# Three constant tiles fetched by another queue, and a new order of all operations, in a windowed attention with a mixture-of-experts attention behind it

## The chip, the cores and the metric

The kernel runs on one core of a Trainium2 chip. The core has TensorE (PE: matmuls; PEld: loading of the stationary operand, which runs beside the matmuls), VectorE (DVE), ScalarE (ACT), GpSimd (POOL) and SyncE (SP), which here only issues transfers. The metric is device time of one execution in microseconds (us), the median of several runs.

## The reference

Two layers over 8 batches, 576 positions and 512 features. The first is attention with 8 heads of 64, a window of 128 positions back and a bias that falls with distance; its output is the input `x` of the second, in which 4 experts each project to 64, do causal attention over all 576 positions, project back to 512, and are summed by the weights of a gate that keeps the best two.

```python
scores = scale * np.matmul(q, k.transpose(0, 1, 3, 2))
mask = (rel >= 0) & (rel < window)                      # window = 128
scores = np.where(mask, scores + bias[None], -1000000000.0)
attn = softmax(scores); x = np.matmul(attn, v)          # then [B, S, 512]

logits = x @ w_gate; topk = best 2 of 4; w = softmax(logits[topk])
for e in range(4):
    q = x @ wq[e]; k = x @ wk[e]; v = x @ wv[e]
    a = softmax(np.where(causal, -1000000000.0, scale * (q @ k.transpose(0, 2, 1))))
    out += w_e * (a @ v @ wo[e])                        # only where e is in topk
```

## The kernel before, in words

The heads go in pairs; pair g belongs to batch g // 4. For each pair the kernel forms blocks of 128 queries against 256 keys: scores on TensorE (tiles `s`, for the first batch `sA`, `sB` and `sC`), mask on VectorE (`COPY_PREDICATED` from `mkt`), bias and row minimum on VectorE (`CUSTOM_DVE_ANT_0` from `tbt`), exponential on ScalarE (`ACTIVATE pA<-pA,nmA`), sums and reciprocals on VectorE (`r`), scaling by the reciprocal on ScalarE or GpSimd (`pA<-pA,r`), transposition on TensorE with the identity `idt` as an operand (`tA`, `tB`, `tC`, `t`), splitting of the transposed block by the mask `tmt` on VectorE together with a plain copy on ScalarE or VectorE (both into `paA`, `pa`), and the product with the values `vt` (`xA`, `xB`, `xt`). The result is kept as a rounded part and a remainder (`xh`). The second layer multiplies these with rounded weights `WH` and their remainders `WL` (`qk`, `v`), forms causal scores (`ms`, `msl`), transposes their exponentials with `idt` (`mt`), and so on to the output.

The four pairs of the first batch are a special case, so that work starts before whole rows have arrived. Their rows come in two halves. `fetch(g, m, 0)` (L313) fetches the first halves of queries and keys of m pairs from g on, one transfer of 128 KB for each of the two heads of a pair, into the tiles named `e`; in a listing these are `e<-in_hd 64x2x256`. One of them, of pair 0, is issued by ScalarE, the others by SyncE. `fetch(g, 2, 1)` and `fetch_tl` (L342) fetch the second halves and the tails of the queries of two pairs: `e<-in_hd 128x2x128`, `e<-in_hd 64x2x256`, `e<-in_rd 128x2x320`, `e<-in_hd 64x2x256`. `fetch_v` (L346) fetches values, `wload` (L991) a chunk of weights of 386 KB (`wst`), and for c = 4 the output weights `wo` of 512 KB and the causal bias `mtt` of 200 KB.

`half_units(0)` (L1206) emits the work on first halves: scores `sA`, probabilities `pA`, transposes `tA`, products `xA`. `half_units(1)` emits that on second halves: the tail scores `sC`, whose operands come from the transfer `e<-in_rd 128x2x320`, the scores `sB`, and what follows. `wprep` rounds weights beside it, and the first projections `qk` come right behind.

None of these calls issues anything. They record operations in a list (`_Rec`); an operation with two possible engines is recorded by `any()` with both. `plan()` (L158) then decodes a string of numbers, `ORDER`, each of which names an operation and which of its two engines takes it, and L1276 issues them in that order. So every operation has line 1276 in the profile, and the order within each engine is that of the string. A negative number stands for a fill: a matmul of a zero tile `QZm` into a scratch tile (`warm`), whose result nobody reads. The string before has 6482 entries, 13 of them fills.

Transfers that SyncE and ScalarE issue use eight semaphores in rotation, in the order of the string: before a transfer can be issued, the one eight places ahead of it must have landed. `tbt` is the bias tile, fetched by ScalarE at the start; `mkt[:, :P]` is computed from it by VectorE, `mkt[:, P:]` is fetched and used for the tail scores `sC` alone.

Of the kernel before, what the change touches and what calls it, by code (L numbers as in the profile page):

```python
# [21 lines left out]
E = 4  # L22
# [21 lines left out]
    "M{knlU;enW`?ZG?lAn6Gq9@&24)v~;9?K{UR@E+cn5@0hfIkteCV<kS27h@8)K-HlyQ3O>Gw;7Q*Bb8cDoYLaKlARd-1pPV8`&D80YI-a81*`>"
    "S|0`I3!aLF^LbWN>ipdF>av(oL>9q&+)z`O6iKN|&?vpWnMpWXUG}#fOepP&qb*xFEZhp1>pj-H?zeiB6Wt2&@qr32JkwQ}pCHNen7;ERaJ=x0"
    "Ei3P1FF>9rB~_(LQ-MONw)Y2MY{HQ<HUYVAw9&MT`39MJehJnkkpk~3fKr3*>h#rBN2ePJbEPl+FgK|*#hOr7YV(N8v<gFxBin9tW@>MEq|Pi%"
    "^L^p^;5aPW6sS{lV??PL9WwNEskM(k8R&<U#__)HzHUd3ZXdvC=$y(eeD7CpeP7aOAI$3qmb$ykp|b(?3|{ML?J(@8Dch#P^8@nUiLw2=zX{_i"
    "ID@D(FgDR22&d@pc&)o{J9*{t2Ub!<w|=bY{`a<AD;|&qb;hptgiuhM*yuF;;75rsK9}1#r_;NWEi>+g&8{36O3EvkV74^Mg;{gDVj(P39+!xV"
    "M~&Hmy+eD(QI)vRTII>j%6ibtmnV(t>P4f5nyr8TqLpbnKG2RsLGj?QBv)gp+gVTj!V^>B+!1qnrn6V$FYb1Vr^Y0U<D1221;s-xZF}9CbyaW2"
    "Z8x_^7He9f4M~1+Pf2+~-axc6(NL$;&s&S8nnR3aeg<H=Bo&TMg%kcx*$VUrRwlGCG@u#m2rf)(rG37!A>|X_t2p(ISd&vsTkGbkie%l?*81N+"  # L50
    ")dt}y<@&Cy5V^WW!7FX-PlaYpCB`dQYw8-6FALzLs#gobRcQb5FCg7yEh;T4wPk(sZ7^8U_M6Xw+Aq=RYkQNA8&&&t(T$3#GpMNg+kXp(@4kYN"
    "Kb%rNQ=L^(US87Iea7e~c}3+(k)h)=S)*~P2v(L3=K7jTG_yar(WpyJ-!EuRovKfk2y6WkAsp*5adgV8lBP_(T)aB1Q)!o{!k$+?nw%mUFLPN2"
    "oRDJ=PqlXe$n`lVOKYHus1q}9zGX%|?t+ofMtX3+<jIFr=IJ@u8-4A&*Y@{XG#(Hp<`*hYcVWID6}&#Mm9Gt^tVTD6MnN1@ZnY-C?>-fDWxJA+"
    "FMSH?o1mywmM6dY;l`GdawsWUs;D|RUfvl?kuaXLP)*V<IChHC%PL`gt8CiX+MkjC$d$Ibqdt$n0okyzB`u>lbG5lZ(VbNj$pv?R@KDn3*kZKK"
    "uvH_)LG|c#X!P1XOvB(X49F0X5<ri_1}rE;<)GHI>vq+r-7}L7{+7n6^}cTTlrU&)Fz&CI_Wc2!=yb*5S)jfytrfP(x?5cBuFMt)jt9qw6nXIc"
    "tIs{Q^!(pM60a|>3(BlZg|;l1EFNY=-F<dTMq_B?u);sK1A9|fuFr?&iKD;1WVfWs(ZV-(K62Z}NP_;PZ9P?|Qs-<$l^L3xez!>uZs@dnj1~~K"
    "fq!_g)SD=swDudTI{aDIe8u>sI~HoJfBsbY(M=B;6HR3vw+XfwPZAVaeBQ==$VjtB#4==4`K2$9udKCx=Zh)rGie!vjmD2YJAT%Yp!)e$XIkR)"
    "T&Xj6uFX+BXJ|Km?xlia{g)n!&b4-Aq)E1P1-|vx8F?WJ=l-@r-MGx}fJ~ljth&^?Rr9?+hGZx*$yL95-^xI5rg1lavTR~W&S;{hE$AJPBp6@%"
    "(ZMm8tVzjkZ^hFet<2T5qFB4pnJ{<574WW1&2|=VOI=0?C^dt_>Ma-=omKA4uWzMq4%iQ@J16R6{hVzi*_+!n=JW1shET*C%bZ<EMg|l53TFBW"
    "_BY+Vlf@--&^Pqo_mmt4ecsSmej#WFa{^XV3$rwzDRE?Mo^C|*dwBr)X01-2l>E@6@W=Z*vi0(PlgrTn*$8``J^g`P_k5tde;Vf8N=<*^iU#tn"  # L60
    "7%wLDK9Va7mxgPl*6u!|)@FBr^K<XZ(j{HFTAT@4Da#oRV?zN;r1`n8@43JCgAR+w)mUFRvb>`zV?<>WIo&xw{+SKz?ZYS-D%(+#eDS5U3`e7s"
    "_rlfT?4d424q8HEi&&QDfxICR9Kr#wP}iwJU`|b$?Ma=UtMA#>h7HP`q6Vm{y|z44Q&I0x-1zRjLzD!Ql83y$VebM=8V+H4uB7~j|5^$i_y2f#"
    "wd}5csgZUhj5D6@KFdyj@wNS4b7_6q;ctFl)@S2k<Qo)WTayNQI?c860+5<hj^Gqd98R?BgJX$!WerY_!=T#*HOfAB+-x;KkeP|1d~>=qzr-}p"
    "EVZ^YR{rYrDW#@~H~9g2a=h*G?GyFG>*IrwT<w8=X<itquGgwli;Gf@d%TN|+GexXZhh{KCO16$4Hzn{o@@7d_<tL%i44QZf4ptSHj)Fjt>OY3"
    "^bfT(j`lfr2ZyhPhesHR<MAiqy|>-=z0lqo=IYRtA;*v<b!ZNvk@hS{o-om!i<StG(I|C6o7~&h*lS&CZc96D9W;CA);F@R`SLW`Hb_H4LEQn~"
    ";XG}<HLF^0Jpg0FEIjgcIC<{Q>ACGpV|v#BOt+YqcVuhbBUMs+nSDO8q4PN;t!}f~Av<fa7p^~kXX<*+KfO5k&kt{E)xWH}ld<msG*^@#RE{+S"
    "$Ndc{sp0fdfSSI|88h<v=YJUXc_Fu|q<rs*&%s*KQcWbO%-k!v_R_Nf$@VVTvV>bawf1c4O6?CHxOv7N>RdA%kL-fM*lAW5YLqo*Fxg$%ND$2)"
    ";w<3@scU~VJS9w=Uz(m1%RnrXTh~xL+fH;WdDL@@<}}TwC_$>&+>xh*r@~E*wR?w?Galtk{om<^$&9<MSZcFAANh@Or!}+ZENWkxAK!50y3;aH"
    "^mWWNm3A6uqAEtDtSS7&rxr!6A9@}bn3>GEXY|WR=yWF|lJ@BV(s!lBkbUs`o8+njU8M&}0PjGrQ<OP1*`;=O?i<#a<fP;zt;Ux8t6u}4ZMJtI"
    "o&^pq_Jd=8p{um$`NwAc&df1r@A$|ECEyT+w^p<jBcA%lA5;XwSKld0hV3K?f}-e`U$vi2jo6{QB=B!v+RGY7;5j<YPH%y;QI}Ma-+v1BPPZ`8"  # L70
    "+Vsd{v+7+WA%FhTaxV<b>w7xO%rM^l*ds_LB}q0<^RvV<e*-dDZlzRNIppg9=6!AJ?yH|RDEx{U80ekV21Y_f6T`Xt-L|bgS6^?o3mDO~a|Lo7"
    "V$aFZF-lob?~@D;7yROB^kjW&Jp{oNeI69%gEn>a#F>-=V>VubOCA{<K7(-5mP8tcTmKY>2?+0+uD>jq40TlrgXr7Da&GIy2rNxQ$D$}Nd43+I"
    "R@)WQx-MyGe7mo^%?*G1v>m$L`H;E?;$&5F5p|1l>R;|39~{o}^amWu@`7T>t*dUcm6tTtPx4OeHkhmpPuVT}cSk)vJJF5*c=TFr(ZR7?1>2|g"
    "fHKEmbU07uuI<ZJ?YG~IRq_b0qdC`&vaA@g7E2DtHwP*j4ysyZV@j7Pw`<YWINQ7?pE<HERKxz+oJl;qrXCp3Ohfr*sN`qQns0xmuRT4{WZ6tM"
    "1x$srW}6$y$HX;brZdy$*tzsUOJ(HoUpO~=A~uoARyugO>&B9DEfP9?=?X2FRul%I;&4ne^0TKh%u$(g$1j8OtDjja%Wi{+RWbYYp8;0eE6YoQ"
    "n$0bxM!sQ|8<DV;M~^d8g<5&f`#%;aE`W#MpFTE`WA7b+ingup1+=FwPt$CA?M}g2ZKkE=#h+k7vAin&<#mRP)x25zMl>zsuq7zTYfef&s@gm3"
    "Pd@ThR82>B#&$QNM+oPQo@lx~CpnlZ=|Nhk9|lmE911D6VC3)LIdYDUA%B}{Bl(l3I^S7n1pe){)85$ykgFCWWtBJIvK{)1VBBont~VROaFjb|"
    "3@e&z@<Q1I*(s;$){I>F?3(LHyjD4L&3$09)G4y<Szv0TUM?RTlFoF9{f*izlqhVuz7t+`EwW~&GeLqqwYLJ#zc6$6m9N|j8})(yTHPS?LI3|v"
    "U-;T}{=lRvFu8;Hm6DpGL)h;<MHSFUZFP0>PzSV|B7kxw5?!12%-ymE$m_AJL6lcmhXmB-4u~_$_k+3abWP7se*u#-&26xLfYLe0)#m&KxK>*Q"
    "-~9H<T7U9Jb#1h1zx0kr{k!gU->flj+n#pAeb6ZCcE0ohm@dsfK4_|U_lKlTm2#n^T&j5f)(!CPwj7-{r%Y5-`6W(NouCQxJnExURR%a@N^o79"  # L80
    "P-_i^Gb174gU>8RwpFJ`d7k5ge95)b$&eZLLZXWNYa!9>-o$Kv`$R9m(@%kVE$s_W==4JaZGp5lUst!j3Z#l)X%kA7mb8d;Pvoer&a%DZv${Q%"
    "xa(Tt7C@^#r~i0#TIS$&ruc*7qeIp+p2>Q`J3SiDvT5Lf52ztj)~463`5U4ellT6i?Hy0%R>~&_(vtT~8za5h>E<QBNgQrj@D8i?h0|8BWPsBK"
    "!Yq4z$GF)6US7s>GE_C^FnzkoYAZA86g$Bet*DX=l`f?r6ck2!D~<Y-zLv;YWV*q=e8$u1yZdarLeHwyI_y6A$z^M*I9+8bO==x4DE$6^d3}td"
    "1TDOywX$Sp*0E-mYnNAHS=r|^B!X1)=Wjcen#G;tjRej9%YVXX-pOno-3}?FFy;=-Ht3rJ;i=6)Ye!Yof#zw>->o)gZSTJNxWYA%aNMI?TUiq="
    "mmGK3{qnU&xZxZ1D4WV#Iy<1I&O3bdJ=3T2(2z9}NX$gJX6<BRF+Hr<jvPi&E9v-+?^N7!Ge|N9wpB}j6!gm4vJYw3*|4gAZ+4<=eB5L2e(2H0"
    "joikKXlhN4B3EJEMBv?+?QGa;Ks2gv`pi93K~+z4n>b?n@=f~*l1wMeuaBxD_gx(xJluoJ-+`0C0Km7N<BmVnf~y|L->B6;@soqBX{104mlq?m"
    "J-tj5BoD4K47k%4W|QuH2|n}0E+POg6=lNc28LR9;JIfOt6c{5m7jyTBlC_Aj-ogPM-$`0o$A`{o*aBiFu!CAo}#?u$Vr&hAc_pwHk*bWcGNx7"
    ">3#SWK;mla=om7Yxh8n(X%rb2BlBu^m%+F#SzBIx_8HOgYScK4AU3+y3cB&2q5m}3t&_a}l2t6bwl6N~+9+#0mMXlyvex_mwW_nnU#3&Qo_2&M"
    "I^2_d<U`#py+QY8f~0K$)*pDK5+?J}>bH|eha#OlDelgisVYa3J0zT5%5`5u+3O5j<m^xq6)~AERQHbu_tTBnVAr7uPY6dQI(s@x%H^X8K2SDv"
    "{_~^NX(0xdBg-d|lhpE(g}!cgLE`CASGA{aR^P1=t__V2jg}-TKKX7?7bE=vSAY9~zxD@4P+hB9KieB`7dM$~y5Zmb;baO>?n9{#l7sjBpsb~H"  # L90
    "N{aL=D3hZn2D!5($U6zGx0S(3(n@hY9PXv2xIjGb@+O3|Q&L5y#hlsKon^}u?tbJE<Ci|%EL7Dtof&U^u-dnB@8+YULkUxv9SM?o<*B;vl~;>V"
    "MVD?UPnC}HIzv12OD1c7z+&$d7BjWC-}(5H{(-)f^1RwpuQBWNGY=wA!>upNl$vZ<EJn&==etjT{}1Wr^e_BkH*BArf#%)n+RaK?WqPm<w3~Xb"
    "v$F>@=(%07wr5+dDX(0duC!aU2Rbv{_-7fYL6Z<nU#c8}z0{cj_~fTMo!Q1c&zWl!qMc2$`K6<DV|dX6izn(rlXU|5!jW?vw#?NxA+(6Ckwr^r"
# [1270 lines left out]
```

## Time and profile before

| | |
|---|---|
| median of 3 runs | 545.17 us (545.03 to 545.23) |
| the profiled execution | 545.23 us |
| its span in the profile | 543.5 us, so 1.73 us lie around it |
| granted TensorE clock, mean over the span | 1.00 of full speed |
| busy: TensorE, VectorE, ScalarE, GpSimd | 532.0, 451.4, 424.7, 348.8 us |
| DMA moved | 72.99 MB, mean 134 GB/s |

The times of single instructions, waits and transfers are those of the profiled execution. "Busy" counts an engine as busy while an instruction runs on it; matmuls overlap each other, so the durations of successive rows can overlap too.

### The profile page before, as it was taken

How to read it: one execution, taken by the hardware profiler on the slowest of the kernel's cores; microseconds unless marked ns; L12 is line 12 of the kernel's file. 1: busy time of each engine (PE TensorE's matmuls, PEld its weight loads, DVE VectorE, ACT ScalarE, POOL GpSimd, SP SyncE). 2: the span in 40 equal slices, each digit the busy share in tenths (PEclk: the TensorE clock that was granted, in tenths of full speed). 3: DMA queues.
4: the chain of work that ended last, by engine and by line, in shares of the span. 5: the costliest groups of instructions: out<-in, count | busy, mean ns of one | idle time of the engine just before them, and what ended most of it. 6: DMA issues, size and time to landing. Idle time of an engine off the chain costs nothing.

```text
span 543.5 us, 13708 instructions
## 1 busy us (share of the span) xinstructions
PE 532.0 (98%) x4353; PEld 453.9 (84%) x4353; DVE 451.4 (83%) x1945; ACT 424.7 (78%) x1477; POOL 348.8 (64%) x591
## 2 busy tenths in 40 slices
...
GB/s 201 252 189 109 155 74 145 132 163 160 200 128 98 175 143 239 157 59 199 141 123 201 119 202 149 148 107 175 162 156 169 81 161 24 76 21 2 19 60 98
DMA packets 30376, 72.99 MB, mean 134 GB/s; under 512 B 3168, under 2 KB 11360, under 8 KB 30304
## 3 DMA queue, kind: packets, MB, share of 16 engines
...
q10 hardware_dynamic: 880, 0.59, 0.4%
q14 instruction: 37, 0.30, 0.2%
HBM read 62.67 MB, written 9.44 MB: 133 GB/s over the span
## 4 chain that ended last, share of the span: by engine, by line
PE 92%; DVE 3%; DMA 3%; issue 1%; SPq 0%; ACTq 0%; ACT 0%; DVEq 0%
PE qk L1276 19%; PE s L1276 11%; PE v L1276 10%; PE o L1276 9%; PE x L1276 8%; PE ms L1276 7%; PE mt L1276 7%; PE ma L1276 7%; PE t L1276 5%; PE msl L1276 2%; PE mal L1276 2%; PE xt L1276 1%; DMA e<-in_rd 1%; PE mtl L1276 1%; DVE pa L1276 1%; DMA tbt<-in_tb 1%
## 5 line engine op out<-in xcount | busy, mean ns | idle before, releaser
L1276 POOL TENSOR_TENSOR h<-r,h 64x512 fp32r<-64x512 f32 x96 | 122.9, 1282 | 16.7 <-DMA r<-in_rd 9.9
L1276 PE MATMUL qk<-xh,WH 128*128 128x288 f32 (+2 forms) x512 | 123.0, 312 | 0.4 <-DVE ot L1276 0.3
L1276 ACT ACTIVATE p<-p,nm 128x128 f32<-128x128 f32 x252 | 99.3, 396 | 14.4 <-DVE nm L1276 12.8
L1276 PEld LDWEIGHTS qk<-xh,WH 128*128 128x128 f32 x512 | 85.0, 189 | 5.2 <-issue 1.6
L1276 POOL TENSOR_SCALAR mp<-mp,mr,w 128x512 f32<-128x512 f32 (+3 forms) x128 | 76.1, 604 | 16.9 <-DVE mr L1276 9.8
L1276 ACT ACTIVATE mp<-mp,mnm 128x256 f32<-128x256 f32 (+3 forms) x128 | 71.1, 557 | 13.5 <-DVE mnm L1276 12.9
L1276 PE MATMUL qk<-xh,WL 128*128 128x288 f32 (+2 forms) x256 | 76.8, 307 | 0.0
L1276 PE MATMUL s<-h 128*128 128x256 f32 x336 | 72.8, 299 | 0.0
L1276 POOL TENSOR_SCALAR p<-p,r 128x128 f32<-128x128 f32 x131 | 47.4, 368 | 36.6 <-DVE r L1276 13.2
L1276 PE MATMUL ms<-KHm,QSm 128*128 128x256 f32 (+2 forms) x224 | 69.0, 359 | 0.1
L1276 DVE TENSOR_TENSOR pa<-t,tmt 128x512 f32<-128x512 f32 (+2 forms) x84 | 64.3, 773 | 5.6 <-PE t L1276 3.7
L1276 PE MATMUL v<-WH,xh 128*128 128x260 f32 x288 | 65.2, 294 | 0.0
L1276 ACT COPY mpt<-mt 128x384 f32<-128x384 f32 (+1 forms) x84 | 44.1, 534 | 26.6 <-PE mt L1276 25.1
L1276 PE MATMUL mt<-idt,mp 128*128 128x128 f32 x320 | 60.9, 273 | 0.0
L1276 DVE CUSTOM_DVE_ANT_0 mp<-ms,mtt 128x256 f32<-128x256 f32 (+2 forms) x96 | 52.4, 552 | 8.1 <-PE ms L1276 7.5
L1276 PEld LDWEIGHTS s<-h 128*128 128x128 f32 x336 | 53.3, 189 | 3.7 <-PE ma L1276 0.4
L1276 DVE CUSTOM_DVE_ANT_0 p<-s,tbt 128x128 f32<-128x128 f32 x204 | 53.2, 284 | 1.9 <-issue 0.2
L1276 PE MATMUL x<-pa,vt 128*64 128x256 f32 x448 | 51.6, 359 | 0.1
L1276 DVE COPY_PREDICATED s<-mkt,s 128x256 f32<-128x256 int32 (+2 forms) x140 | 45.0, 330 | 6.3 <-PE s L1276 4.4
L1276 PE MATMUL t<-idt,p 128*128 128x128 f32 x252 | 49.7, 273 | 0.1
L1276 PEld LDWEIGHTS v<-WH,xh 128*128 128x128 f32 x288 | 48.2, 189 | 1.9 <-issue 1.3
L1276 ACT ACTIVATE p<-p,r 128x128 f32<-128x128 f32 x121 | 45.4, 396 | 5.0 <-DVE r L1276 3.7
...
## 6 DMA issues: line engine op xcount, KB each, us to landing
...
tl<-in_hd SPq DMA_DIRECT2D x24, 64.0 KB, 3.4
...
```

The costliest lines, as they stand in the source:

```text
L1276: getattr(getattr(tc.nc, e), m)(*a, **k)
```

## The change

The three fetches of constants leave ScalarE's queue. `idt` (64 KB) is issued by SyncE between the fetch of pair 0 and those of pair 1 in the code, `tmt` (64 KB) behind the first halves of pairs 2 and 3, and `mkt[:, P:]` (32 KB) behind the last weight chunk. And the string `ORDER` is another one, for the whole program: 6477 entries, 8 of them fills, and with the same operations otherwise (6469 distinct ones in both). Some operations are on their other engine: three plain copies into `paA` in the first batch's first halves go to VectorE, and roundings of the weights `WH` to ScalarE in their place.

```diff
 ORDER = (
-    "c-pmjeOzl-m3GcKD<8LTO>Ck`P1>ZAX{bblB^_uJC#gvVZ_<J#l_<Fb78G7V!G@N!V1q&nQ>b7;!9s-!N=BH0npm(w!2yMzprFKp1_gx*dg%)m"
...
+    "c-pmje^_g0m2URlD?iRjG^wOFjG$1HHnC8XmQ0C;Hfh5&oRT(aVGIfiHYil6P@zrQ#DWC{1q(K@(1HgXXoH0gSTY3#4N4T0D2z}+;T9ZF7{P+V"
...
     zero()
     fetch(0, 1, 0)
     nc.scalar.dma_start(tbt[:, 3], tb[:, 3])
-    nc.scalar.dma_start(idt, ident)
-    nc.scalar.dma_start(tmt, tm)
-    nc.scalar.dma_start(mkt[:, P:], mk[:, P:])
     nc.vector.tensor_scalar(mkt[:, :P], tbt[:, 3, 0, :], -1.0e6, None, op0=ALU.is_lt)
...
     warm()
+    nc.sync.dma_start(idt, ident)
     fetch(1, 1, 0)
     fetch_v(0, 0)
     fetch(2, 2, 0)
+    nc.sync.dma_start(tmt, tm)
     fetch_v(1, 0)
     fetch_v(2, 0)
     wload(0)
     fetch_v(3, 0)
     for c in range(1, 4):
         wload(c)
+    nc.sync.dma_start(mkt[:, P:], mk[:, P:])
     aseq, marks = attn_units()
```

SyncE's queue at the start of the program, before. `e_107` holds the rows of pairs 0 and 1, `e_111` those of pairs 2 and 3; `vt_110`, `vt_112`, `vt_113` and `vt_115` are the values of pairs 0 to 3.

```order
L1276 DMA e_107<-in_hd 64x2x256 x3
L1276 DMA vt_110<-in_vd 128x256
L1276 DMA e_111<-in_hd 64x2x256 x4
L1276 DMA vt_112<-in_vd 128x256
L1276 DMA vt_113<-in_vd 128x256
L1276 DMA wst_114<-in_wall 128x772
L1276 DMA vt_115<-in_vd 128x256
L1276 DMA wst_116<-in_wall 128x772
L1276 DMA wst_117<-in_wall 128x772
L1276 DMA wst_118<-in_wall 128x772
L1276 DMA e_107<-in_hd 128x2x128
L1276 DMA e_107<-in_hd 64x2x256
```

The same place of SyncE's queue after, as far as the third of the moved transfers.

```order
L1276 DMA e_107<-in_hd 64x2x256 x2
L1276 DMA vt_110<-in_vd 128x256
L1276 DMA e_111<-in_hd 64x2x256 x4
L1276 DMA tmt<-in_tm 128x256
L1276 DMA vt_112<-in_vd 128x256
L1276 DMA vt_113<-in_vd 128x256
L1276 DMA wst_114<-in_wall 128x772
L1276 DMA vt_115<-in_vd 128x256
L1276 DMA wst_116<-in_wall 128x772
L1276 DMA wst_117<-in_wall 128x772
L1276 DMA wst_118<-in_wall 128x772
L1276 DMA mkt<-in_mk 128x64
```

Ahead of these rows stand one `e_107<-in_hd 64x2x256` and `idt`, and behind them the second halves `e_107<-in_hd 128x2x128` and so on as before. So SyncE issues three more transfers ahead of the first transfer of a second half. Further on, the transfers of the tail of a later pair (`tl`, 64 KB) and of `mtt` (200 KB) now stand ahead of most of the second halves of pairs 2 and 3, and `wo` (512 KB) ahead of the last values; before, they came behind these.

TensorE from the last block of the first half of pair 2 to the first projections, before. `tA_147` are the transposes of pair 3, `xA_145` the product of pair 2, `sC_163` and `sC_157` the tail scores of pairs 1 and 0, `sB` the second-half scores of pair 0.

```order
L1276 MATMUL sC_163<-e_107 128x192
L1276 MATMUL warm_109<-QZm 128x256
L1276 MATMUL sC_157<-e_107 128x192
L1276 MATMUL sB_0_155<-e_107 128x256
L1276 MATMUL sB_1_156<-e_107 128x256
L1276 MATMUL sB_0_155<-e_107 128x256
L1276 MATMUL sB_1_156<-e_107 128x256
L1276 MATMUL xA_145<-paA,vt_113 64x256 x2
L1276 MATMUL xA_145<-paA,vt_113 64x128 x2
L1276 MATMUL tA_147<-idt,pA_133 128x128 x4
L1276 MATMUL qk_0_0_165<-xh_131,WH 128x256 x2
```

The same place on TensorE after.

```order
L1276 MATMUL tA_147<-idt,pA_133 128x128 x4
L1276 MATMUL warm_109<-QZm 128x256 x3
L1276 MATMUL sC_163<-e_107 128x192
L1276 MATMUL warm_109<-QZm 128x256
L1276 MATMUL sC_157<-e_107 128x192
L1276 MATMUL sB_0_155<-e_107 128x256
L1276 MATMUL sB_1_156<-e_107 128x256
L1276 MATMUL sB_0_155<-e_107 128x256
L1276 MATMUL sB_1_156<-e_107 128x256
L1276 MATMUL xA_145<-paA,vt_113 64x256 x2
L1276 MATMUL xA_145<-paA,vt_113 64x128 x2
```

The four transposes `tA_147` moved from behind the scores `sB` to a place ahead of the tail scores `sC`, with three fills between; the first projections `qk` now follow the product `xA_145` directly. On VectorE the reciprocal for pair 3, by which `pA_133` is scaled ahead of these transposes, stood behind a rounding (`WH`) and a remainder (`WL`) of weights, and now follows directly on the sum that it is taken of.

## Rows read from the trace of the kernel before

**Rows 1.** The first part of the profile's page (busy time of each engine, its share of the span, number of instructions) and the shares by engine of the chain of work that ended last.

```profile
PE 532.0 (98%) x4353; PEld 453.9 (84%) x4353; DVE 451.4 (83%) x1945; ACT 424.7 (78%) x1477; POOL 348.8 (64%) x591
...
PE 92%; DVE 3%; DMA 3%; issue 1%; SPq 0%; ACTq 0%; ACT 0%; DVEq 0%
```

**Rows 2.** Busy time of each engine by stretch of the span (start and end of the stretch in us: its length, then for each engine its busy time and, in brackets, how many instructions; then the granted TensorE clock, the busy share of the 16 DMA engines and the GB/s that they moved).

```profile
10.00:15.00 5.00, 4.51 (x22) 3.26 (x20) 3.96 (x24) 3.94 (x18) 2.09 (x6) 1.00 0.93 305
15.00:20.00 5.00, 3.78 (x30) 2.74 (x31) 3.20 (x15) 4.13 (x19) 3.52 (x8) 1.00 1.11 283
20.00:25.00 5.00, 5.00 (x41) 3.57 (x40) 4.21 (x21) 3.74 (x16) 3.17 (x6) 1.00 1.04 263
...
60.00:80.00 20.00, 19.86 (x163) 16.46 (x164) 18.52 (x83) 15.71 (x63) 16.65 (x30) 1.00 0.25 76
80.00:100.00 20.00, 19.65 (x143) 15.46 (x145) 18.34 (x81) 17.68 (x65) 15.66 (x28) 1.00 0.60 197
100.00:200.00 100.00, 99.92 (x848) 87.59 (x844) 86.04 (x383) 82.86 (x285) 73.72 (x119) 1.00 0.44 145
200.00:300.00 100.00, 99.71 (x819) 85.49 (x816) 87.90 (x371) 84.91 (x293) 70.76 (x110) 1.00 0.49 155
```

**Rows 3.** Waits of TensorE over the whole span (engine, tile and line that waited, what it waited for: us in total, times, longest).

```profile
PE sA L1276 <- DMA e<-in_hd: 4.2, 1, 4.2
PE sA L1276 <- PE sA L1276: 0.8, 1, 0.8
PE sC L1276 <- DMA e<-in_rd: 0.7, 1, 0.7
```

**Rows 4.** Timeline of SyncE's queue from 0 to 25 us: start us, duration us of the row's issues together, the transfer, how many issues.

```profile
0.74 2.09 SPq L1276 DMA_DIRECT2D e<-in_hd  x3
...
3.50 3.94 SPq L1276 DMA_DIRECT2D e<-in_hd  x4
7.48 1.07 SPq L1276 DMA_DIRECT2D vt<-in_vd  x2
8.59 0.43 SPq L1276 DMA_DIRECT2D wst<-in_wall  x1
...
9.59 1.33 SPq L1276 DMA_DIRECT2D wst<-in_wall  x3
10.96 1.34 SPq L1276 DMA_DIRECT2D e<-in_hd  x2
12.35 0.59 SPq L1276 DMA_DIRECT2D e<-in_rd  x1
```

**Rows 5.** Waits of SyncE's queue from 0 to 25 us, columns as in rows 3.

```profile
SPq L1276 <- DMA tbt<-in_tb: 1.4, 1, 1.4
```

**Rows 6.** Timeline of ScalarE and its queue from 0 to 25 us: start us, duration us, instruction, count, and in brackets the idle time before it and what ended that.

```profile
6.20 0.34 ACTq L1276 DMA_DIRECT2D tmt<-in_tm  x1
6.58 0.44 ACTq L1276 DMA_DIRECT2D idt<-in_ident  x1
8.06 0.40 ACT L1276 ACTIVATE pA<-pA,nmA 128x128 f32<-128x128 f32 x1 [1.45 <-DVE nmA L1276]
...
12.99 0.33 ACTq L1276 DMA_DIRECT2D mkt<-in_mk  x1
13.87 0.37 ACT L1276 COPY paA<-tA 128x256 f32<-128x256 f32 x1 [0.70 <-PE tA L1276]
...
20.05 0.99 ACT L1276 ACTIVATE pA<-pA,r 128x128 f32<-128x128 f32 x3 [0.51 <-DVE r L1276]
```

**Rows 7.** Timeline of TensorE's matmuls from 0 to 25 us, columns as in rows 6.

```profile
15.85 1.09 PE L1276 MATMUL warm<-QZm 128*128 128x256 f32 x7
...
19.82 0.56 PE L1276 MATMUL sC<-e 128*128 128x192 f32 x2 [0.69 <-DMA e<-in_rd]
...
20.76 1.13 PE L1276 MATMUL sB<-e 64*128 64x256 f32 x8
...
22.62 0.66 PE L1276 MATMUL tA<-idt,pA 128*128 128x128 f32 x4
23.04 0.48 PE L1276 MATMUL qk<-xh,WH 128*128 128x256 f32 x2
```

**Rows 8.** Timeline of TensorE's weight loads from 0 to 25 us, columns as in rows 6.

```profile
5.94 0.50 PEld L1276 LDWEIGHTS sA<-e 64*128 64x128 f32 x2 [0.81 <-DMA e<-in_hd]
6.63 1.40 PEld L1276 LDWEIGHTS sA<-e 64*128 64x128 f32 x8 [0.20 <-DMA e<-in_hd]
```

**Rows 9.** Timeline of VectorE from 0 to 25 us, columns as in rows 6.

```profile
10.79 0.16 DVE L1276 TENSOR_REDUCE r<-sm 128x4 f32<-128x8 f32 x1 [0.91 <-ACT pA L1276]
...
18.79 0.16 DVE L1276 TENSOR_REDUCE r<-sm 128x4 f32<-128x8 f32 x1 [1.08 <-ACT pA L1276]
...
20.78 0.35 DVE L1276 COPY_PREDICATED sC<-mkt,sC 128x64 f32<-128x64 int32 x2
```

**Rows 10.** From the view of the tile wst (the weight chunks), 0 to 40 us: the time from issue to landing of its four fetches.

```profile
DMA to landing us min/median/max: 4.4/5.1/6.4
```

**Rows 11.** From the view of all DMA issues: destination and source, queue, number of issues, KB each, median us from issue to landing.

```profile
tl<-in_hd SPq DMA_DIRECT2D x24, 64.0 KB, 3.4
...
mtt<-in_mt SPq DMA_DIRECT2D x1, 200.0 KB, 3.1
```

More of the change, by code (lines that the diff above doesn't have):

```diff
@@ L44 @@
[L44 to L93, printed above, removed]
@@ new lines @@
+    "2nx#mzHjdU=ZyDx=KgW>gd}J0Z+}15df&C)wT=!z1>}|L66sT2DWz!!O<ihwZ>mev6-srP8L3+3s#Oh1tFtrqd!^OlLy5ao3%S}Mv3V^RpS|WT"
+    "?ow}fAOCQDeA~(Gj}+Ib;Qf4kLQz@o6Zg5=!CUK)R=&)8I?p3@`JQ+r|J@Illte5+(Dmm_(vMTW@ca{RHye*X@N>)YeeY!WVE(kYzSVd6wqJfA"
+    "#XA7-&8J`H@m@*EzU}@QXY*0Zqkk*Z>Sqh}9i^WyzQbLbs&EG;RSnH80dMWMzjx|shCh5-_rM#uSxHt~b<T}nXx*0F#INhrg?sB{ZJkDQQ)~Kf"
+    "o{5%K0<5~03?8fbOE1KgYxmyqdW$aAH{bfu2lLcL&=Sb#DmB;SJak7x>-TR87}dTw|G+^Llt_J()9LGL4YfmcovP`&we*bjL`IaJ0id4P0cc2Z"
+    "WR(CUD$teu%CaHTqj^`T|LW|oe&WM&Rh&v&n}5SgHB6&WGN`X<Q0Y?o#xgSoLrt|>?LkWbpt4Mt;&Ve@4kTwxwG<gEAHQFem*($=OK;7NCiSc-"
```

141 lines of the change are left out of this document (93 added, 48 removed).

## Prediction

> **What bounds the kernel now.** I read the page's busy times first, then the chain that ended last, then the busy times by stretch, then who waits for what at the start. TensorE is busy 532.0 of 543.5 us, and 92% of the chain is TensorE [rows 1]. The reader should see that no other engine comes near: the next is VectorE at 83%. By stretch, TensorE lacks 5.00 − 4.51 = 0.49 us between 10 and 15 us and 5.00 − 3.78 = 1.22 us between 15 and 20 us, and between 60 and 300 us only 0.14 + 0.35 + 0.08 + 0.29 = 0.86 us together [rows 2]. So behind the first 25 us the time is that of the matmuls themselves. Their operations are the same after the change, apart from fills, so a new order can win or lose there only small slips. At the start the limits are others. TensorE waits 4.2 us for the very first rows, which the change leaves alone, 0.8 us among the first scores, and 0.7 us for the fetch behind the tail scores `sC` [rows 3]; and the 16 DMA engines are busy 0.93 and 1.11 of the time from 10 to 20 us [rows 2], so a transfer there waits for transfers.
>
> **The change part by part.** The sum is made against the profiled execution, 545.23 us (its span of 543.5 and 1.73 around it). That is 0.06 above the median of the runs, 545.17, which is nothing beside the terms.
>
> *ScalarE loses three issues*, 0.34 + 0.44 + 0.33 = 1.11 us [rows 6]. All three lie in gaps that something else ends: `tmt` and `idt` in the 1.45 us before 8.06, ended by VectorE's minima, `mkt` in the 0.70 us before 13.87, ended by the transposes. So this gives 0; were it all on the path it would be −1.11.
>
> *SyncE gains the same three.* Each is followed separately.
>
> `idt`, 0.44 us at some 1.55, pushes the rows of pair 1 and all behind them back by 0.44. TensorE's weight loads wait for these rows, 0.81 us before 5.94 and 0.20 before 6.63 [rows 8], so the scores of pair 1 come 0.44 later. Their next users are VectorE's minima. There is cover behind them, since VectorE waits 0.91 us for ScalarE at 10.79 [rows 9]. I take 0; without that cover it costs 0.44.
>
> `tmt`, 0.34 us, comes behind the first halves of pairs 2 and 3. Here SyncE already stands still 1.4 us until `tbt` has landed [rows 5]. The end of that wait can be read: the row of four fetches ends at 3.50 + 3.94 = 7.44, and two of these, at some 0.60 each with gaps of 0.04, come behind the wait, which puts its end at 7.44 − 2 × 0.60 − 0.04 = 6.20, where ScalarE starts on `tbt` too [rows 4, 6]. With `idt` ahead in the rotation of semaphores, the fetch that must wait for `tbt` is the last of the four and no longer the last but one. So `idt` is swallowed by that wait, and behind it come one fetch, `tmt` and two of values: 6.20 + 0.60 + 0.34 + 1.07 and three gaps of 0.04 give 8.33 for the first weight chunk, where it was 8.59.
>
> `mkt`, 0.33 us, comes behind the last weight chunk. From the first chunk to the second halves it took 10.96 − 8.59 = 2.37 [rows 4]; with `mkt` and a gap of 0.04 that is 8.33 + 2.37 + 0.37 = 11.07, later than before by 0.11. The transfer that matters is the third of these, `e<-in_rd`, issued at 12.35 [rows 4], by turn now at 12.46. But its partner eight places ahead in the rotation is now the first weight chunk, and no weight chunk landed in less than 4.4 us [rows 10]: 8.33 + 4.40 = 12.73. That is +0.38 for the transfer for which `sC` waits with 0.69 us of idle time at 19.82 [rows 7], so TensorE starts `sC` 0.38 later. Bounds: 0, if the crowded DMA engines end the transfer at the same time anyhow; +1.11, if every issue that SyncE gained shows. I take +0.38, which is read from the nearest rows.
>
> What `mkt` is needed for, the mask of `sC`, VectorE reaches at 20.78 [rows 9]; a fetch issued before 11.07 leaves it more than 9 us. That costs nothing.
>
> *The transposes `tA_147` move ahead of `sC`.* Before, they took TensorE from 22.62 to 23.04, 0.42 us [rows 7], in a stretch where it is busy all the time (5.00 of 5.00 from 20 to 25 us [rows 2]). Now they can lie in the time in which TensorE waits for `sC`'s operands. That is −0.42, if their probabilities are ready by 20.2. Before they were not: ScalarE scaled them from 20.05 to 21.04, after VectorE's reciprocal, whose sum came at 18.79 [rows 6, 9]. Two things bring them forward. The reciprocal now follows its sum directly, and ScalarE has given two copies of 0.37 us ahead of them to VectorE. VectorE has room, being busy 3.20 of 5.00 us from 15 to 20 us [rows 2]. Bounds: −0.42, and 21.04 − 20.20 = +0.84, if the scaling ends where it did and `sC` stands behind it. I take −0.42.
>
> *Five fills fewer.* Seven of them took 1.09 us together, 0.16 each, at 15.85, in a stretch where TensorE waits [rows 2, 7]. They pass waiting time and do not make it: 0; if all five had been on the path, −0.78.
>
> *The order of the rest.* No view of the profile before shows which slips the new order closes or opens. From above, the 0.86 us of idle time between 60 and 300 us [rows 2] is what is shown to be there; narrower slips, in which one matmul follows another a little late, do not count as idle, and I allow as much again and more, to −2.0. From below, a reshuffled program could open what this one has closed: +1.5, somewhat under twice 0.86. I take three quarters of the shown idle time, −0.65, since the change keeps every operation and only places it anew.
>
> Sum: −0.42 + 0.38 − 0.65 = −0.69, and 545.23 − 0.69 = **544.5 us**.
>
> **One rule beside this.** In the first 20 us the transfers of both queues together fill the DMA engines [rows 2]. The Trainium skill, "DMA: Bandwidth & Descriptors", section "Issuing engines are not separate DMA queues", says the same: transfers started by SyncE, ScalarE or GpSimd run on the same 16 engines, and spreading them over issuers saves only issue time. By that rule the move can win no bandwidth and turns two issuers' time into one's; the trace agrees with the first part by its shares of 0.93 and 1.11. By it alone, with nothing from the order, the sum would be 545.23 + 1.11 = 546.3.
>
> **The rivals.**
>
> *(a) The new order closes the narrow slips too.* For it: 0.86 us is only what shows as idle, and in a kernel at 98% TensorE a slip is as good as a wait. Against it: the stretches from 100 to 300 us have just 0.37 us left to show [rows 2]. It would give −0.42 + 0.38 − 1.8, about 543.4.
>
> *(b) It does nothing that reaches the end.* The start's gain is eaten by a next wait, the order's slips balance: 545.2. For it: all three moved transfers were covered before, and TensorE's share is the same matmuls. Against it: the transposes do leave a stretch in which TensorE has no gap.
>
> *(c) SyncE's queue becomes the limit of the second halves.* The three issues cost 1.11, and `tl` and `mtt`, 64 + 200 = 264 KB [rows 11], now go ahead of most of the second halves of pairs 2 and 3; at the 283 GB/s of 15 to 20 us [rows 2] that is 0.96 us of a DMA that is already full. Place: TensorE before `sC` and before the second-half scores `sB`. Price: 1.11 + 0.96 = 2.07, less 0.42 for the transposes, +1.65: 546.9. It decides from the point where some 1.5 of the 2.07 us reach TensorE. For it: the 0.69 us wait shows that TensorE there hangs on a transfer. Against it: of the 1.11 us SyncE's own wait for `tbt` swallows most, and before `sB` of the later pairs TensorE has projections to do, as the full stretch from 20 to 25 us shows.
>
> **How the numbers follow.** The forecast gets 0.42, with a range of its own of 544.1 to 545.0; (a) 0.30, (b) 0.12, (c) 0.16. A measurement of this kernel can tell about 0.2%, 1.09 us, from no change, so "faster" means below 544.08 and "slower" above 546.26. Faster is (a) and the lower edge of the forecast, 0.38; slower is (c), 0.16, as the others stay below; the rest, 0.46, is no difference. The range reaches into (a) and, above, to where (c) would begin to show: 543.0 to 546.3.
>
> **What would show it.** In the profile after: `idt` on SyncE at about 1.55; the weight loads of pair 1 at about 6.4 and 7.1; no transfer of constants on ScalarE behind `tbt`; the first weight chunk issued at about 8.3 and `e<-in_rd` at about 12.7; `tA_147` before `sC`, and `sC` at about 20.2; the first `qk` at about 23.0, where it was 23.04; less than 0.86 us of idle time on TensorE from 60 to 300 us. The prediction is wrong if `sC` waits beyond 20.7 for transfers or stands behind `tA_147`, if TensorE has new waits for rows after 25 us, or if the time is below 543.5 with a start no better than before: then the order of the rest was worth more than I read.

## The result: slower, and not the same twice

The changed kernel takes 548.75 us (median of 6 runs, 546.41 to 549.39) where the kernel before, on the same chip, takes 545.10 (6 runs, 544.88 to 545.53): a ratio of 1.0058, 95% interval 1.0036 to 1.0079. The six lie 3.0 us apart, those of the kernel before 0.65; in the later sessions, with 16 to 29 executions each, the kernel before spreads over 2.1 to 2.5 us, so the spread says less than the median. The profiled execution is the fastest of the six, 546.41.

The page's busy times and the chain of that execution:

```profile
PE 532.0 (98%) x4348; PEld 453.3 (83%) x4348; DVE 462.1 (85%) x1959; ACT 422.2 (78%) x1471; POOL 347.4 (64%) x583
...
PE 89%; DVE 5%; SPq 2%; DMA 1%; POOL 1%; ACT 1%; issue 1%; DVEq 0%; ACTq 0%; POOLq 0%
```

TensorE is busy for the same 532.0 us as in [rows 1], but its share of the chain fell from 92% to 89%, and VectorE's rose from 3% to 5%. By stretch (columns as in [rows 2]):

```profile
15.00:20.00 5.00, 2.56 (x18) 1.65 (x19) 3.85 (x10) 2.79 (x10) 4.32 (x9) 1.00 1.10 280
20.00:25.00 5.00, 5.00 (x38) 3.79 (x38) 4.71 (x22) 2.33 (x11) 2.76 (x4) 1.00 0.79 217
...
60.00:80.00 20.00, 20.00 (x162) 16.75 (x161) 18.51 (x84) 15.30 (x59) 13.16 (x28) 1.00 0.12 34
80.00:100.00 20.00, 19.80 (x144) 15.51 (x143) 18.06 (x79) 19.65 (x73) 15.39 (x26) 1.00 0.56 187
100.00:200.00 100.00, 99.70 (x838) 86.85 (x838) 90.70 (x389) 81.97 (x287) 70.38 (x107) 1.00 0.47 148
200.00:300.00 100.00, 99.97 (x824) 86.23 (x819) 87.93 (x367) 82.28 (x283) 72.31 (x115) 1.00 0.48 152
300.00:400.00 100.00, 99.86 (x836) 86.98 (x834) 89.40 (x385) 76.68 (x271) 74.56 (x120) 1.00 0.48 151
400.00:500.00 100.00, 99.27 (x832) 87.69 (x831) 83.35 (x337) 76.06 (x263) 58.21 (x101) 1.00 0.29 90
```

From 60 to 300 us the idle time of TensorE shrank to 0.00 + 0.20 + 0.30 + 0.03 = 0.53 us, where [rows 2] had 0.86. But from 300 to 500 us there are now 0.14 + 0.73 = 0.87 us, where the kernel before had none:

```profile
300.00:400.00 100.00, 100.00 (x832) 87.33 (x832) 86.64 (x377) 78.35 (x278) 70.43 (x109) 1.00 0.45 148
400.00:500.00 100.00, 100.00 (x835) 88.39 (x834) 82.29 (x334) 75.25 (x258) 60.06 (x107) 1.00 0.28 90
```

And from 15 to 20 us TensorE is busy 2.56 us, not 3.78. The five fills fewer, at 0.16 us each, are 0.8 of that; the rest is work that now lies elsewhere.

The start itself went nearly as worked out. SyncE's queue:

```profile
1.55 0.82 SPq L1276 DMA_DIRECT2D idt<-in_ident  x1
...
8.55 0.43 SPq L1276 DMA_DIRECT2D wst<-in_wall  x1
...
10.92 0.58 SPq L1276 DMA_DIRECT2D mkt<-in_mk  x1
...
12.88 0.60 SPq L1276 DMA_DIRECT2D e<-in_rd  x1
```

and TensorE's matmuls:

```profile
17.39 0.55 PE L1276 MATMUL tA<-idt,pA 128*128 128x128 f32 x3 [0.26 <-ACT pA L1276]
...
19.91 0.56 PE L1276 MATMUL sC<-e 128*128 128x192 f32 x2 [1.62 <-DMA e<-in_rd]
...
22.71 0.74 PE L1276 MATMUL qk<-xh,WH 128*128 128x256 f32 x4
```

The transfer behind `sC` is issued at 12.88 (12.35 in [rows 4]), `sC` starts at 19.91 (19.82 in [rows 7]), and the first `qk` at 22.71, a third of a microsecond earlier than 23.04. So in this execution the loss lies behind the start. Of TensorE's longest waits behind the one for the first rows, only the third, `s` for VectorE's `mr`, lies there:

```profile
PE sC L1276 <- DMA e<-in_rd: 1.6, 1, 1.6
PE tA L1276 <- POOL pA L1276: 1.3, 2, 0.7
PE s L1276 <- DVE mr L1276: 0.7, 1, 0.7
```

### The profile page after: what moved, and what is told of

The parts are those of the page before. It is cut to its first block, busy times and chain, and to the rows that moved or that the text cites. A ratio compares the mean times of both kernels' runs of the same rounds, so it can differ in the third digit from the quotient of the medians.

```text
span 544.6 us, 13672 instructions
## 1 busy us (share of the span) xinstructions
PE 532.0 (98%) x4348; PEld 453.3 (83%) x4348; DVE 462.1 (85%) x1959; ACT 422.2 (78%) x1471; POOL 347.4 (64%) x583
## 4 chain that ended last, share of the span: by engine, by line
PE 89%; DVE 5%; SPq 2%; DMA 1%; POOL 1%; ACT 1%; issue 1%; DVEq 0%; ACTq 0%; POOLq 0%
PE qk L1276 18%; PE s L1276 10%; PE v L1276 10%; PE o L1276 9%; PE x L1276 7%; PE mt L1276 7%; PE ms L1276 7%; PE ma L1276 7%; PE t L1276 4%; PE msl L1276 2%; SPq L1276 2%; PE mal L1276 2%; PE mtl L1276 1%; DVE pa L1276 1%; PE xt L1276 1%; DMA e<-in_rd 1%
## 5 line engine op out<-in xcount | busy, mean ns | idle before, releaser
L1276 POOL TENSOR_SCALAR mp<-mp,mr,w 128x128 f32<-128x128 f32 (+3 forms) x128 | 76.6, 610 | 20.9 <-DVE mr L1276 12.3
L1276 PE MATMUL qk<-xh,WL 128*128 128x288 f32 (+2 forms) x256 | 78.0, 310 | 0.0
L1276 ACT ACTIVATE mp<-mp,mnm 128x384 f32<-128x384 f32 (+3 forms) x128 | 71.0, 557 | 6.5 <-DVE mnm L1276 4.9
L1276 PE MATMUL s<-h 128*128 128x256 f32 x336 | 71.3, 298 | 0.9 <-DVE mr L1276 0.7
L1276 PE MATMUL ms<-KHm,QSm 128*128 128x256 f32 (+2 forms) x224 | 66.6, 356 | 0.0
L1276 ACT COPY mpt<-mt 128x512 f32<-128x512 f32 (+1 forms) x78 | 41.4, 536 | 24.4 <-PE mt L1276 24.0
```

Of the source, the lines that this page charges most:

```text
L1276: getattr(getattr(tc.nc, e), m)(*a, **k)
```

## The experiments

All times are medians; each ratio is to the kernel before in the same session, with its 95% interval.

| run | what it is | us | ratio |
|---|---|---|---|
| changed kernel | | 548.75 | 1.0058 (1.0036 to 1.0079) |
| e1_after_again | the same | 548.02 | 1.0053 (1.0038 to 1.0068) |
| e2_moves_only | order before, fetches on SyncE | 545.25 | 0.9998 (0.9988 to 1.0007) |
| e3_after_first60 | new order to 60 us, then the old | 546.90 | 1.0029 (1.0018 to 1.0040) |
| e4_before_first60 | old order to 60 us, then the new | 549.23 | 1.0070 (1.0053 to 1.0088) |
| e5_fills | e3 and 18 fills | 546.28 | 1.0018 (1.0009 to 1.0028) |
| e6_ws | changed, `ws` in another form | 546.42 | 1.0023 (1.0011 to 1.0034) |
| e7_G | changed, one `G` earlier | 546.82 | 1.0031 (1.0018 to 1.0043) |
| e8_all | changed, edits of e5, e6, e7 | 544.63 | 0.9985 (0.9974 to 0.9995) |
| e9_before_ws | before, `ws` in another form | 544.99 | 0.9994 (0.9985 to 1.0003) |
| e10_ws_G | changed, edits of e6 and e7 | 545.25 | 1.0001 (0.9989 to 1.0012) |
| e11_back | e8, fetches on ScalarE | 545.04 | 0.9999 (0.9990 to 1.0008) |
| e12_after_fills | changed, the 18 fills alone | 547.65 | 1.0038 (1.0021 to 1.0056) |

**The changed kernel again.** No edit. Expected:

> The changed kernel as it is, profiled a second time. Its six times spread over 3 us (546.4 to 549.4) where those of the kernel before spread over 0.7, and its profile was of the fastest of them, whose first 23 us went as forecast. Theory A (a wait on a transfer or on GpSimd that is there in some executions only, behind the first 60 us): a profile of a 548 to 549 us execution shows it as one or two new waits of 1 to 3 us together. Theory B (the start: SyncE's queue, held up by the fetch of wo at 25 us): the extra 2 to 3 us lie before 60 us. Theory C (the clock): the extra time lies in stretches with a granted clock under 1.00.

The profiled execution took 547.76, and its waits hold one that the first profile has not:

```profile
PE ms L1276 <- DVE nm L1276: 1.5, 1, 1.5
...
PE s L1276 <- DVE mr L1276: 0.7, 1, 0.7
```

Who made VectorE late? Its own timeline of this execution (start us, duration us) shows two small operations that take many times their length:

```profile
313.45 2.05 DVE L1276 TENSOR_TENSOR G<-lg 128x80 f32<-128x80 f32 x1
...
404.99 1.09 DVE L1276 TENSOR_SCALAR ws<-ws 128x5 f32<-128x5 f32 x1
406.00 0.68 DVE L1276 TENSOR_TENSOR pa<-t,tmt 128x512 f32<-128x512 f32 x1
```

GpSimd's timeline shows what runs beside them:

```profile
313.30 0.78 POOL L1276 DMA_DIRECT2D h<-in_hd  x1 [1.29 <-DMA r<-in_rd]
314.11 1.28 POOL L1276 TENSOR_TENSOR h<-r,h 64x512 fp32r<-64x512 f32 x1
...
404.76 1.29 POOL L1276 TENSOR_TENSOR h<-r,h 64x512 fp32r<-64x512 f32 x1
```

Both end within 0.11 us of the end of `h<-r,h`: 313.45 + 2.05 = 315.50 against 314.11 + 1.28 = 315.39, and 404.99 + 1.09 = 406.08 against 404.76 + 1.29 = 406.05. In the first profile of the changed kernel the same `G` took its normal time, though it began as short a while behind the issue of the transfer. VectorE and GpSimd there:

```profile
313.83 0.23 DVE L1276 TENSOR_TENSOR G<-lg 128x80 f32<-128x80 f32 x1
```

```profile
313.67 0.78 POOL L1276 DMA_DIRECT2D h<-in_hd  x1 [1.24 <-PE mt L1276]
```

So theory A has its shape: a wait behind GpSimd that is there in some executions. Theory C is not to be seen in this trace, whose granted clock is 1.00 in every stretch.

**The moves alone.** The order before, in which the three entries stand where the change puts them on SyncE:

```diff
-    nc.scalar.dma_start(idt, ident)
-    nc.scalar.dma_start(tmt, tm)
-    nc.scalar.dma_start(mkt[:, P:], mk[:, P:])
+    nc.sync.dma_start(idt, ident)
+    nc.sync.dma_start(tmt, tm)
+    nc.sync.dma_start(mkt[:, P:], mk[:, P:])
```

> The order before, with only the three fetches moved to SyncE, at the places in its queue that the change gives them. Theory A and C: the moves are not the cause, 545 within 0.5. Theory B: part of the loss shows, 546 or more, with the wait of sC longer than the 0.7 us before. My forecast of the terms: +0.38 for the later fetch of sC's operands and no transposes to win it back, 545.5.

545.25, no difference (the interval reaches from −0.65 to +0.38 us). In its trace the wait of `sC` is longer, as forecast,

```profile
PE sC L1274 <- DMA e<-in_rd: 1.1, 1, 1.1
```

and nothing of it is to be seen in the time. What the change is named after does not make the loss; the order does.

**The order in two halves.** Two kernels, each with one kernel's order up to the first score matmul of pair 6 and, behind it, what is left in the other's (here e3, in words; e4 is the other way round):

```diff
 ORDER = (
-    the changed kernel's list
+    its entries up to the first matmul into s6_1, then all others as the list before has them
```

> The changed kernel's order up to the first score matmul of pair 6 (at some 60 us), then what is left in the order before. Theory A: the loss is gone, 545 within 0.7, and the spread with it. Theory B: the loss stays, 547 to 549. Theory C says nothing of it unless the clock falls in one part.

> The other way round: the kernel before up to the first score matmul of pair 6, fetches on ScalarE, and then what is left in the changed kernel's order. Theory A: the loss stays, 547 to 549, with a spread of 2 to 3 us. Theory B: 545 within 0.7.

Neither theory alone held: 546.90 and 549.23, both slower. The profile of e3 shows why its half costs. By stretch:

```profile
15.00:20.00 5.00, 2.67 (x18) 1.76 (x19) 3.92 (x10) 2.82 (x11) 4.28 (x9) 1.00 1.12 272
20.00:24.00 4.00, 4.00 (x21) 2.48 (x20) 3.00 (x12) 0.79 (x3) 1.79 (x3) 0.57 0.93 264
24.00:25.00 1.00, 1.00 (x13) 0.83 (x8) 1.00 (x10) 0.71 (x4) 0.97 (x2) 1.00 0.26 81
```

The granted clock falls to 0.57 of full speed on the mean from 20 to 24 us (1.00 is the level of 2.4 GHz, 0.50 that of 1.2), behind a stretch in which TensorE was busy 2.67 of 5 us. The second-half scores then take twice as long, 2.08 us in place of the 1.13 of [rows 7]:

```profile
21.15 2.08 PE L1274 MATMUL sB<-e 64*128 64x256 f32 x8
```

The first profile of the changed kernel has the same order up to there and a clock of 1.00, so the two can be laid side by side. Against the kernel before, TensorE begins `sC` of pair 1 at −0.03 us in e3 and +0.09 in the changed kernel, so the two are nearly level; the last matmul into `xB` of pair 0, at 31 us, begins at +1.09 and −0.05. The fall costs this execution 1.1 to 1.3 us. e4 carries, besides the waits of the new order, one that the seam made, so its extra 1.2 us over e1 say nothing of the change:

```profile
PE t L1274 <- POOL p L1274: 1.9, 1, 1.9
PE ms L1274 <- DVE nm L1274: 1.5, 1, 1.5
...
PE s L1274 <- DVE mr L1274: 0.7, 1, 0.7
```

**Fills back.** e3's kernel with 18 fills (the order on TensorE, in words):

```diff
+MATMUL warm<-QZm x4
 MATMUL tA (pair 1) x4
...
 MATMUL tA (pair 2) x2
+MATMUL warm<-QZm x4
 MATMUL tA (pair 2) x2
...
+MATMUL warm<-QZm x10
 MATMUL sC
```

> The kernel of e3 (changed order to 60 us, order before behind it; 546.90 against 545.17) with 18 fills more among the first transposes: 4 ahead of tA of pair 1, 4 between the transposes of pair 2, 10 ahead of the tail scores sC, all in time in which TensorE waits. Theory C1 (the idle time between 11 and 20 us lets the granted clock fall to half from 20 to 24 us, as the profile of e3 shows; that is what the five fills had prevented): 545.2 within 0.5, granted clock 1.00 from 20 to 25 us, and less spread. Rival C2 (it is the order of the transposes and transfers that costs 1.7, and the clock comes beside it): 546.5 or more, since fills do no work and only add some 2 us of matmuls.

546.28, part of the way back: the kernel before, run beside it, takes 545.42. The ratios of e3 and e5, 1.0029 and 1.0018, have intervals that overlap. In e5's profile the clock holds:

```profile
15.00:20.00 5.00, 4.20 (x34) 3.25 (x33) 4.26 (x11) 3.38 (x13) 4.18 (x9) 1.00 1.12 259
20.00:24.00 4.00, 4.00 (x30) 2.80 (x28) 3.71 (x17) 0.97 (x5) 1.78 (x4) 1.00 1.08 258
```

In this execution, the slowest of the ten, VectorE is held beside GpSimd once more, at another place. A comparison that normally takes 0.17 us, and GpSimd's row beside it:

```profile
263.96 1.27 DVE L1274 TENSOR_SCALAR cnt<-cnt 128x20 f32<-128x20 f32 x1
```

```profile
263.93 2.60 POOL L1274 TENSOR_TENSOR h<-r,h 64x512 fp32r<-64x512 f32 x2 [2.58 <-DMA r<-in_rd]
```

In the kernel before, the same comparison begins 0.80 us into `h<-r,h`, takes 0.51 us, and no wait of TensorE follows; here it begins 0.03 us into it, and TensorE then waits 0.7 us. In both profiles GpSimd starts `h<-r,h` when the rows `r` land, so there it is a transfer that sets the distance between the two.

**The two operations of VectorE.** e6 changes the form of one small operation (the 1e-9 is left out), e7 moves another ahead of the two before it in VectorE's queue:

```diff
-        nc.vector.tensor_scalar(ws, ws, EPS, None, op0=add)
+        nc.vector.tensor_reduce(ws, ws.unsqueeze(2), AX.X, add)
```

```diff
 TENSOR_TENSOR G<-lg (first of batch 4)
+TENSOR_TENSOR G<-lg (second of batch 4)
 COPY_PREDICATED s<-mkt,s
 TENSOR_REDUCE mx<-lg
-TENSOR_TENSOR G<-lg (second of batch 4)
```

> The changed kernel with one small operation of VectorE in another form, in all 8 batches: the addition of 1e-9 to the sum of the gate's weights, tensor_scalar on a tile in SBUF, becomes a tensor_reduce over one element, which leaves the 1e-9 out. In the profiles this tensor_scalar takes 1.1 us in place of 0.2 at 143 and 405 us, and ends with GpSimd's h<-r,h beside it. Theory D1 (VectorE is held up by GpSimd there, TensorE then waits 0.3 and 0.7 us): both stretches are gone, 0.7 to 1.0 less than the changed kernel's 548.0, so 547.1. Rival D2 (the operation waits for something else, or TensorE finds its next wait at once): the next operation takes the wait over, 548.0.

> The changed kernel with one operation of VectorE moved three places forward: in the batch at 313 us, the second comparison G<-lg, which took 2.05 us in the profile of e1 and 0.23 in the first profile of the changed kernel, both times begun 0.15 us behind the start of GpSimd's transfer h<-in_hd. Theory D1: begun earlier it never meets the transfer, TensorE's wait of 1.5 us at 314 is gone from the executions that had it; these are most, so the median falls by about 1, to 547.0. Rival D2: whatever stands there then is held up instead, and the time stays at 548.0.

546.42 and 546.82: by the ratios e6 gains 1.6 us and e7 1.2 over e1 (e7's interval just overlaps e1's). For e6 that is more than the 0.3 and 0.7 us that showed as idle time on TensorE. In e6's profile VectorE's `ws` takes 0.16 us at both places, and `G`, which e6 leaves alone, is held as before:

```profile
145.01 0.16 DVE L1274 TENSOR_REDUCE ws<-ws 128x5 f32<-128x5 f32 x1
...
314.48 2.05 DVE L1274 TENSOR_TENSOR G<-lg 128x80 f32<-128x80 f32 x1
...
406.01 0.16 DVE L1274 TENSOR_REDUCE ws<-ws 128x5 f32<-128x5 f32 x1
```

GpSimd was at work on `h<-r,h` both times, just as in the changed kernel:

```profile
144.81 1.29 POOL L1274 TENSOR_TENSOR h<-r,h 64x512 fp32r<-64x512 f32 x1
...
405.77 1.30 POOL L1274 TENSOR_TENSOR h<-r,h 64x512 fp32r<-64x512 f32 x1
```

That execution also shows something that the other profiles have not: TensorE waits for rows of pair 4.

```profile
39.24 0.46 PE L1274 MATMUL s<-e 64*128 64x128 f32 x2 [0.38 <-DMA e<-in_hd]
39.90 0.89 PE L1274 MATMUL s<-e 64*128 64x128 f32 x6 [0.20 <-DMA e<-in_hd]
```

SyncE issued these rows from 32.55 us on, as early as in e7's profile (32.58), where TensorE does not wait for them, and its wait of 3.6 us with the fetch of `wo` ahead of them is 3.8 in e7. But the fetches issued from 31 to 36 us landed 6.3 to 7.3 us behind their issue, in e7 3.1 to 4.1. So in this one execution the transfers took longer, and the queue was not late; why they did is not shown.

**All three edits.**

> The changed kernel with the edits of e5, e6 and e7 together. If theories C1 and D1 hold and together are all of the loss: 545.2 less some tenths, with the spread of the kernel before, 0.5 to 1. If the order has a further loss spread over many small slips: 546 or more.

544.63: faster than the kernel before, ratio 0.9985, and the 10 runs lie within 0.91 us. (The kernel before spread over 2.46 us in that session, in 27 executions.) TensorE's waits of this profile, all of them:

```profile
PE sA L1274 <- DMA e<-in_hd: 3.8, 1, 3.8
PE tA L1274 <- ACT pA L1274: 1.0, 3, 0.4
PE tA L1274 <- POOL pA L1274: 0.2, 1, 0.2
```

None is left behind the start. Since e8 has the same order, its trace is the rule against which the others can be laid. How much later than in e8 TensorE begins the last matmul of a product tile (us, from the starts of the matmuls in each trace):

| last matmul of | changed, first profile | e1 | e6 (`ws`) | e7 (`G`) |
|---|---|---|---|---|
| pair 0, at 31 us | −0.47 | −0.44 | 0.25 | 0.28 |
| pair 10, at 136 | −0.45 | −0.48 | 1.30 | 0.26 |
| pair 14, at 201 | 0.16 | 0.06 | 1.30 | 0.84 |
| pair 18, at 266 | 0.45 | 0.13 | 1.27 | 1.02 |
| pair 22, at 331 | 0.58 | 1.87 | 2.90 | 1.14 |
| pair 26, at 396 | 0.44 | 1.73 | 2.75 | 1.01 |
| pair 30, at 463 | 1.39 | 2.63 | 2.71 | 1.90 |
| the end | 1.59 | 2.90 | 2.80 | 2.12 |

Each column steps up where its collisions lie and nowhere else by much: 0.5 to 0.6 between pairs 10 and 14 (`ws` at 143 us; not in e6), 1.6 to 1.7 between pairs 18 and 22 in e1 and e6 (`G` at 314; not in e7, nor in the first profile), 0.9 between pairs 26 and 30 (`ws` at 404; not in e6). A smaller step, 0.1 to 0.3 between pairs 14 and 18 and none in e6, goes with `ws` at 208 us, which is held in the kernel before as well. In e6 the late rows of pair 4 add 1.05 before pair 10.

**What each edit is worth, and what would have done for the kernel before.** e9 is the kernel before with e6's edit, e10 is e8 without the fills, e11 is e8 with the three fetches on ScalarE as before, e12 the changed kernel with the fills alone.

> The kernel before, its order untouched, with the one small operation in the other form (as in e6: tensor_reduce over one element for the addition of 1e-9, which is left out). The profile of the kernel before has one stretched ws<-ws, 1.02 us at 206.65, and 0.29 us without work on TensorE at 208. Theory D1: that goes, 0.3 to 0.45 less, ratio 0.9993. Rival (the form is faster anyhow or changes the rest): more than 0.8 less, and then what e6 and e8 gained is not the new order's.

> e8 without the 18 fills: the changed kernel with the edits of e6 and e7 alone. If the three causes add up: e8's 544.6 plus what the clock and the start cost on the mean of executions without fills, 0.5 to 1.7, so 545.1 to 546.3, with single executions as fast as e8's. If the fills did nothing: 544.6.

> e8 with the three fetches back on ScalarE (tmt and idt behind the first operation on tbt, mkt behind the last weight chunk in the order), everything else as in e8. Theory M0 (the place of the fetches is worth nothing, as e2 showed for the order before): e8's 544.6 within 0.5. Rival M1 (the new order was made for the fetches on SyncE and needs the identity early, since the transposes begin at 11.0 us in it): 545.3 or more.

> The changed kernel with the 18 fills alone, both collisions of VectorE and GpSimd left as they are. If the causes add up: 548.0 less 0.5 to 1.7, so 546.3 to 547.5, and executions with the stretched G<-lg about 1.3 above those without. If the clock was all: 545.2.

The two edits on VectorE together bring the changed kernel from 1.0053 to 1.0001, some 2.8 us; singly they bring 0.0030 and 0.0022, so they add up. The fills bring 0.0015 alone (e1 to e12) and 0.0016 behind the other two (e10 to e8), some 0.8 to 0.9 us; but in both pairs the intervals overlap. e10's executions reach from 543.82 to 547.39, e8's from 544.27 to 545.18, and e10's profile caught the clock at half once more:

```profile
15.00:20.00 5.00, 2.47 (x17) 1.52 (x17) 3.43 (x10) 2.99 (x11) 4.29 (x8) 1.00 1.09 270
20.00:24.00 4.00, 3.69 (x15) 2.57 (x17) 2.52 (x9) 0.79 (x3) 1.73 (x4) 0.57 1.08 268
```

Against e8's trace, TensorE begins the last matmul of pair 0 in this execution 1.22 us later and that of pair 30 1.00 later: all of its loss lies ahead of 31 us.

So of six profiles with the new start and few fills two show the fall, and of the four with 18 fills more none does. The profiles are not all that there is: every execution has a mean granted clock, and e3's and e10's profiled ones, with the fall, stand at 0.997 and 0.995. Of the 44 executions with the new start and few fills, 16 stand at 0.997 or below; of the 38 with 18 fills more, none. In e3 the five low ones take 547.0 us on the mean and the other two 545.85; in e10 the five low ones take 545.95 and the other six 544.82, close to e8's mean of 544.66. In e6 the three low ones take only 0.3 us more. The mean does not say where in an execution the clock fell, and the old start has low ones too: 2 of 4 in e4, and 8 of 72 of the kernel before, which in the session with six of the eight take 0.2 us more. So the fills take the low executions away, and such an execution costs some 1.1 us in e3 and e10. The collisions' share is shown by edit and by trace.

e9 gained 0.0006, as much as the idle time of its one collision says, but its interval holds 1. e11 and e8 differ by 0.0014, from two sessions and with intervals that overlap: whether the new order has any use for the fetches on SyncE stays open.

## Why the prediction was wrong

*The moves of the three fetches* were right in the main: the transfer behind `sC` was issued at 12.88, forecast 12.73, and first weights at 8.55, forecast 8.33. Alone the moves are worth 0.9998; the +0.38 of the sum lies at the edge of that interval and does not show in the changed kernel, whose `sC` starts 0.09 later. SyncE's wait for `tbt` did not come, since `tbt` had landed by 4.59, not 6.20, and the weight loads of pair 1 began at 5.66, forecast 6.4.

*The transposes ahead of `sC`* were right: the four began between 16.80 and 17.66, after 0.34 and 0.26 us of waiting for their probabilities and still well ahead of `sC`, and `qk` began at 22.71, forecast 23.0.

*"They pass waiting time and do not make it: 0"*, the step on the fills, is wrong. It priced a fill by what it occupies. The profile before shows only that with 13 of them the clock held at 1.00; what it does with 8, after 2.5 us of work in 5, no row showed, and I gave it no bound above 0. Measured: 1.1 to 1.3 us in an execution in which the clock falls, and some 0.8 to 0.9 on the median, with overlapping intervals.

*"I take three quarters of the shown idle time, −0.65"* is the step that failed most. It took the idle rows from 60 to 300 us as the sum of what the order could win, and a reshuffle as a small thing either way: its bound of +1.5 came from the same 0.86, and e1's collisions alone make twice that. The idle time there did fall, 0.86 to 0.53. But the new order laid operations of VectorE beside GpSimd's `h<-r,h` at places where TensorE depends on them at once: 0.5 to 0.6 us at 143, 0.9 at 404, and 1.6 to 1.7 at 314 in some executions. The sum nearly closes. In e1 these steps make 0.54 + 1.74 + 0.90 = 3.18; less the 0.44 by which its start lies ahead of e8's, that is 2.74 of the 2.90 us by which it ends behind e8. In the first profile 0.61 + 0.95 − 0.47 = 1.09 of 1.59; the 0.5 left is spread over smaller steps, 0.29 of it between pairs 14 and 18. Without the collisions and with the fills, the new order comes out near what I had put down for it: e8's median lies 0.79 below that of the kernel before, and the forecast was −0.69. That is luck in part: e8 has three edits of which the forecast knew nothing, and the one on `ws` gains 0.3 us on the kernel before as well, though not clear of noise.

One such collision stood in the profile that I had read from, at VectorE's `ws<-ws`, 1.02 us at 206.65, with 0.29 us of idle time on TensorE behind it. I counted the 0.29 as something to win, and did not ask what had made a sum of five columns take a microsecond.

The change was also larger than its description. Decoded, the two strings put 384 of the 6469 operations on their other engine, about as many in each tenth of the program, not only the copies and roundings named there; VectorE is busy 462.1 us where it was 451.4. That is not where the loss lies, since e8 keeps all 384 and is not slower.

*The rivals.* (c) had the right sign by a mechanism that did not come. The rows of a second half, behind which `sC` waits, let it wait longer, 0.8 to 1.8 us in the six profiles with the new start and few fills, yet the first `qk` behind it begins at 22.5 to 23.2 in the four of them whose clock held (23.04 before). TensorE waited for later rows, 0.6 us at pair 4, in one of the six, and there the transfers landed late and SyncE's queue did not issue them late. (a) and (b) did not come.
